# A chunked linear-attention kernel: state kept block-diagonal, TensorE's tile modes counted in the order of work, and spare matmuls at the start

## The chip, the cores and the metric

The kernel runs on one core of one Trainium2 chip. The metric is the device time of one launch in microseconds. The kernel before takes 105.71 us, the median of three runs (104.99 to 107.63). The profile was taken in another run of the same kernel, which took 102.53 us and whose profiled span is 100.8 us.

## The reference

Two parts follow each other. The first is a linear attention with a decaying state, for 4 sequences, 8 heads, 768 steps and head size 48. The second sends each of the 3072 resulting rows of 384 numbers through the best two of eight small adapters.

```python
def _attn_ref(r, k, v, w, u):
    state = zeros((B, H, D, D))
    for t in range(S):
        cur = einsum('bhd,bhe->bhde', u[None] * kt, vt)
        y[:, :, t] = einsum('bhd,bhde->bhe', rt, state + cur)
        state = wt[:, :, :, None] * state + einsum('bhd,bhe->bhde', kt, vt)

def _moe_ref(x, w_gate, A, B):            # E = 8 adapters of rank 16
    logits = x @ w_gate
    topk = the two largest;  w = softmax over those two
    out = x + sum over the two of  w * ((x @ A[e]) @ B[e])
```

The kernel handles a sequence as six tiles of 128 steps, 24 tiles in all. Within a tile, with cumulative sums of log w, the output has three terms: what the tile's own earlier steps give (a masked 128 by 128 matrix per head), what the state at the tile's start gives, and the diagonal term with u.

## The kernel before

Each step of the work is a small function of a tile number, and a long list, PLAN, gives the order in which all of them are issued; every engine then runs its own instructions in that order. A star in PLAN lets a copy change sides between ScalarE and VectorE. The host lays r and k out with head dimension on partitions, two heads to a tile of 128 partitions: head 0 of a pair in partitions 0 to 47, head 1 in 64 to 111.

The steps that matter here, with cuts marked:

```python
def cs(t):      # cumulative sums of log w: full-array matmuls, 4 or 8 of 128 columns
    ...
def expP(t):    # eP = exp(cs) on ScalarE; expN: exp(-cs)
def multR(t):   # rT = r * eP, multK: kT = k * eN, both on VectorE
def rku(t):     # r * k on GpSimd; dg(t): its sum with u by 4 matmuls of 2 columns
def dgev(t):    # dg of two tiles copied out of PSUM by ScalarE
def dv(t):      # v * dg on GpSimd: the diagonal term

def load_v(t):
    n = VGROUPS[t]
    v16 = io.tile([L, n, HD], FP16, name=f"v16_{t}")
    nc.gpsimd.dma_start(out=v16, in_=v[:, t:t + n])
    ...

def amm(t):     # a_ps[s, head, t] = k . r, 8 matmuls on 48 rows of the array
    ...
def aev(t):     # at = a_ps * mask, on VectorE

def kv(t):      # the state's sum over tiles, in PSUM
    if t % NC == 0:
        nc.tensor.matmul(S_acc, lhsT=zeros[:, 0:128], rhs=zeros, start=True, stop=False, ...)
    for p in range(P):
        for g in range(2):
            b = g * 64
            nc.tensor.matmul(S_acc[b:b + D, p], lhsT=st[t]["kn"][:, 2 * p + g], rhs=st[t]["v16"][:, 2 * p + g],
                             start=False, stop=True, ...)

def sev(t):     # the state copied to SBUF
    sb = wk.tile([128, P, D], BF16, name="S_sb", bufs=3)
    copy("ACT", sb, S_acc)
    st[t]["S"] = sb

def ymm(t):     # the three terms of the output
    y_ps = ring([128, P, 128], F32, "y_ps")
    s_ = st[t]
    for p in range(P):                                     # diagonal term
        nc.tensor.matmul(y_ps[:, p, :], lhsT=pair(s_["dv"], p), rhs=ident16, start=(p == 0), stop=False, ...)
    if t % NC > 0:
        for p in range(P):
            for g in range(2):                             # state's term
                b = g * 64
                nc.tensor.matmul(y_ps[b:b + D, p, :], lhsT=st[t - 1]["S"][b:b + D, p], rhs=s_["rT"][b:b + D, p], ...)
    for p in range(P):
        for g in range(2):                                 # the tile's own steps
            b = g * 64
            nc.tensor.matmul(y_ps[b:b + D, p, :], lhsT=s_["v16"][:, 2 * p + g], rhs=s_["at"][:, g * P + p], ...)
    s_["y_ps"] = y_ps

# yev: y_ps to xT (ScalarE); lg: gate logits; gate, gmax, gsel, z, zw, zT, zTev: the two best adapters,
# their weights and the first projection, for batches of 4, 4, 4, 4, 4, 3 and 1 tiles;
# d: x plus the second projection; oev: copy to SBUF; store: to DRAM
```

Memory for sums: [...] One bank, s_ps, is shared by the state (192 columns), dg (a slot for each of 24 tiles) and the gate logits lg (16 slots). The tiles kn_ps, y_ps, z_ps, zT_ps and d_ps take turns in two banks ("ring"). Input tiles have 12 buffers for r and k, 8 for w, and one of its own for every group of v.

Of the kernel before, what the change touches and what calls it, by code (L numbers as in the profile page):

```python
# [8 lines left out]
F32 = mybir.dt.float32  # L9
# [16 lines left out]
    setup.0 load_wb.0 adapters.0 load_wa.0 ln1.0 ln.0 cs.0 load_rk.0 expN.0 expP.0 casts.0 rku.0 multK.0 cs.1  # L26
    load_w.2 load_rk.1 ln.2 kT.0 load_rk.2 load_w.4 load_v.0 multR.0 expN.1 amm.0 expP.1 cs.2 multK.1 multR.1 dg.0
    expP.2 aev.0 load_rk.3 kT.1 load_v.1 rku.1 expN.2 dg.1 amm.1 dgev.1 ln.4 kev.1* multR.2 cs.3 kev.0 dv.0 expP.3
    multK.2 ymm.0 kT.2 kv.0 load_rk.4 rku.2 aev.1 expN.3 dg.2 multR.3 cs.4 amm.2 load_w.6 rku.3 load_rk.5 yev.0
    load_rk.6 sev.0 dv.1 multK.3 kv.1 dg.3 kev.2* load_v.4 expN.4 kT.3 dgev.3 dv.2 aev.2 expP.4 ymm.1 kev.3* sev.1  # L30
    amm.3 dv.3 cs.5 multK.4 rku.5 multR.4 yev.1 lg.0 lg.1 expN.5 aev.3 kv.2 expP.5 ymm.2 amm.4 load_w.8 ln.6 multK.5
    cs.6 adapterB.0 load_rk.7 multR.5 kT.4 yev.2 rku.4 sev.2 expP.6 dg.5 load_rk.8 rku.6 aev.4 ymm.3 multR.6
    load_w.10 kv.3 dg.4 expN.6 lg.2 kev.4* dgev.5 amm.5 dv.4 load_rk.9 multK.6 cs.7 sev.3 dg.6 kv.4 yev.3 lg.3 kT.6
    expN.7 ymm.4 gate.3 expP.7 sev.4 dv.5 aev.5 amm.6 kev.6 gmax.3 aev.6 ln.8 load_rk.11 kv.6 ymm.5 yev.4 cs.8
    load_rk.10 gsel.3 multK.7 sev.6 load_w.12 rku.7 multR.7 z.3 castB.0 yev.5 dg.7 expN.8 kT.7 zw.3 multK.8 expP.8
    amm.7 dgev.7 rku.8 dv.6 multR.8 load_v.8 load_rk.12 cs.9 aev.7 dg.8 load_w.14 kev.7* ln.10 dv.7 kT.8 expN.9
    expP.9 load_rk.13 multK.9 ymm.6 lg.5 kv.7 kev.8* amm.8 cs.10 sev.7 yev.6 rku.9 multR.9 aev.8 expN.10 lg.4
    multK.10 lg.6 zT.3 expP.10 multR.10 ymm.7 dg.9 zTev.3* cs.11 load_w.16 yev.7 amm.9 expN.11 aev.9 load_rk.14
    rku.11 rku.10 ln.12 lg.7 load_rk.15 dg.11 dg.10 expP.11 d.1 load_v.12 dgev.9 gate.7 dv.8 multK.11 kT.9 dv.9
    load_rk.16 kev.9* oev.1 cs.12 expN.12 amm.10 kv.8 kT.10 gmax.7 ymm.8 multR.11 dgev.11 gsel.7 load_rk.17 rku.12  # L40
    kev.10 multK.12 d.0 sev.8 kv.9 expP.12 multR.12 yev.8 cs.13 z.7 sev.9 oev.0 aev.10 ln.14 rku.13 ymm.9 zw.7 lg.8
    dv.10 expN.13 rku.14 dv.11 amm.11 expP.13 zT.7 cs.14 multK.13 zTev.7 yev.9 multR.13 ln.16 kT.13 load_w.20 kv.10
    d.3 lg.9 expN.14 load_w.18 dg.13 kev.13 expP.14 oev.3 ymm.10 aev.11 yev.10 multK.14 dg.12 kT.12 cs.15 amm.12 d.5
    sev.10 multR.14 kev.12* aev.12 dgev.13 rku.15 dg.14 ymm.11 expN.15 oev.5 lg.10 d.2 amm.13 kv.12 load_rk.18
    expP.15 dg.15 dv.13 multK.15 yev.11 oev.2 dv.12 sev.12 rku.16 kT.14 multR.15 cs.16 dgev.15 kev.14* load_v.16
    kv.13 kT.15 load_rk.19 lg.11 aev.13 expP.16 ymm.12 load_rk.20 kev.15 expN.16 amm.14 load_rk.22 gate.11 d.6
    load_rk.21 rku.17 sev.13 cs.17 dg.16 multR.16 yev.12 oev.6 multK.16 d.7 expP.17 ymm.13 gmax.11 gsel.11 oev.7
    kv.14 dv.15 z.11 expN.17 aev.14 multK.17 sev.14 amm.15 dv.14 yev.13 ln.18 dg.17 d.4 kv.15 zw.11 kT.16 oev.4
    load_w.22 cs.18 load_rk.23 multR.17 zT.11 sev.15 dgev.17 aev.15 kev.16* rku.18 expN.18 zTev.11 ymm.14 amm.16
    expP.18 ymm.15 multK.18 dg.18 cs.19 ln.20 yev.14 dv.16 lg.14 yev.15 kT.18 kv.16 multR.18 expN.19 lg.13 lg.12  # L50
    dv.17 aev.16 lg.15 d.10 kev.18* amm.17 load_v.20 expP.19 multK.19 ymm.16 cs.20 rku.19 sev.16 store.5 aev.17
    oev.10 rku.20 multR.19 gate.15 d.9 yev.16 gmax.15 expN.20 ymm.17 oev.9 kv.18 store.9 gsel.15 expP.20 store.2
    yev.17 multK.20 amm.18 d.8 oev.8 dg.19 cs.21 kT.19 store.3 dgev.19 aev.18 sev.18 expN.21 z.15 kev.19* dv.18
    amm.19 ymm.18 multR.20 expP.21 yev.18 lg.16 kv.19 zw.15 ln.22 zT.15 multK.21 rku.21 dg.21 dg.20 kT.21 zTev.15
    kev.21* aev.19 d.13 store.1 lg.18 multR.21 cs.22 kT.20 oev.13 sev.19 dv.19 kev.20 rku.23 amm.20 expN.22 ymm.19
    dgev.21 d.15 rku.22 store.6 dv.20 aev.20 lg.17 store.7 expP.22 dg.22 yev.19 multR.22 dg.23 kv.20 d.12 oev.15
    lg.19 amm.21 oev.12 dv.21 gate.19 multK.22 dgev.23 dv.23 sev.20 ymm.20 d.11 store.13 store.0 yev.20 oev.11
    aev.21 cs.23 store.10 dv.22 expN.23 gmax.19 kv.21 d.14 oev.14 sev.21 amm.22 ymm.21 yev.21 gsel.19 aev.22 z.19
    ymm.22 lg.20 multK.23 lg.21 expP.23 zw.19 yev.22 zT.19 lg.22 store.4 store.15 gate.22 store.12 multR.23 kT.22
    zTev.19 amm.23 d.17 kev.22* gmax.22 kv.22 aev.23 gsel.22 store.8 oev.17 d.18 sev.22 z.22 oev.18 zw.22 ymm.23  # L60
# [23 lines left out]
def kernel(  # L84
# [190 lines left out]
    def dg(t):  # L275
        for p in range(P):
            nc.tensor.matmul(dg_ps[:, t, 2 * p:2 * p + 2], lhsT=st[t]["rku"][:, p], rhs=w16[:, p, ER + E:],  # L277
                             start=False, stop=True, skip_group_check=True)
# [47 lines left out]

    def sev(t):
        sb = wk.tile([128, P, D], BF16, name="S_sb", bufs=3)
        copy("ACT", sb, S_acc)
        st[t]["S"] = sb  # L330

    def ymm(t):
# [5 lines left out]
        if t % NC > 0:  # L338
            for p in range(P):
                for g in range(2):  # L340
                    b = g * 64
                    nc.tensor.matmul(y_ps[b:b + D, p, :], lhsT=st[t - 1]["S"][b:b + D, p], rhs=s_["rT"][b:b + D, p],  # L342
                                     start=False, stop=False, skip_group_check=True)
# [156 lines left out]
```

## Time and profile before

| | us | share of the span |
|---|---|---|
| span of the profiled run | 100.8 | |
| TensorE matmul (PE) busy, 1505 matmuls | 85.9 | 85% |
| TensorE weight load (PEld) busy | 64.6 | 64% |
| ScalarE (ACT) busy | 72.3 | 72% |
| VectorE (DVE) busy | 72.0 | 71% |
| GpSimd (POOL) busy | 57.4 | 57% |
| DMA, moved | 25.19 MB | 250 GB/s in the mean |

Busy time of TensorE is a union of overlapping matmuls whose ends are modelled, so it says that TensorE had something under way, not that it streamed at its peak. In the profile's groups a matmul bears the rows and columns of the array that it uses: 128\*128 is the whole, 48\*128 the k and r products of one head, 128\*48 those with v of one head as weights, 48\*48 the state's term of one head. The granted clock has no record before about 5 us, and the page prints full speed there; the eight spare matmuls of 512 columns that the kernel already has at its start stand 0.43 us apart in the timeline.

The largest single groups are the masked copy of the attention matrix on VectorE (24 times 1218 ns), r times k on GpSimd (24 times 1088 ns) and the copies and exponentials of 128x512 on ScalarE (about 590 ns each, 72 of them).

### The profile page before, as it was taken

Reading aid. Unit: us, or ns where it says so; the run is one execution under the profiler, and the core shown is the slowest. Engines: PE = TensorE matmul, PEld = TensorE weight load, DVE = VectorE, ACT = ScalarE, POOL = GpSimd, SP = SyncE. Lnnn points to the kernel's source line nnn. Section 1 sums busy time; section 2 is a strip of 40 time slices with the busy share of each in tenths; the row PEclk is TensorE's granted clock in tenths of the full one; section 3 lists DMA queues with packets and bytes.
Section 4 is the critical chain, followed back from the end, with each engine's and each line's share of the span. In section 5 each row is a group of like instructions: output and inputs, shape, how many; then the busy total and the mean of one; then the engine's idle time right before and its main releaser. Section 6 shows DMA issues by size and latency. Waiting matters only on the chain.

```text
span 100.8 us, 3702 instructions
## 1 busy us (share of the span) xinstructions
PE 85.9 (85%) x1505; PEld 64.6 (64%) x1505; DVE 72.0 (71%) x145; ACT 72.3 (72%) x165; POOL 57.4 (57%) x95
## 2 busy tenths in 40 slices
PE   3935672999999998957999999999999999999840
PEld 1313661778588787735887788767787777866520
DVE  6205697076688989997689979896987995984410
ACT  5243583574859998994998899899887977465730
POOL 6105706959406989708995965996159849021300
PEclk9996555555579999999999999999999999999999
DMA  2999999999999999999998355009075285304272
GB/s 60 266 304 367 420 362 299 408 411 327 350 420 404 419 418 409 299 353 293 380 418 328 125 56 110 0 0 147 15 266 205 85 300 205 128 6 156 112 260 100
DMA packets 10097, 25.19 MB, mean 250 GB/s; under 512 B 1120, under 2 KB 4704, under 8 KB 10080
## 3 DMA queue, kind: packets, MB, share of 16 engines
q1 hardware_dynamic: 9072, 22.60, 58.9%
q0 software_dynamic: 1008, 2.36, 13.2%
q8 instruction: 11, 0.18, 0.7%
q14 instruction: 6, 0.05, 0.2%
HBM read 22.60 MB, written 4.72 MB: 271 GB/s over the span
## 4 chain that ended last, share of the span: by engine, by line
PE 68%; DMA 15%; POOL 5%; ACT 4%; DVE 2%; issue 1%; SPq 1%; DVEq 0%; POOLq 0%
DMA v<-in_v_dram 8%; PE y_ps L347 8%; PE a_ps L298 7%; PE y_ps L336 7%; PE y_ps L342 7%; DMA rk_in<-in_rk_dram 6%; PE z_ps L393 6%; PE d_ps L425 5%; PE cs_ps L238 5%; PE cs_ps L240 5%; PE kn_ps L310 4%; PE s_ps L324 4%; PE d_ps L427 3%; PE s_ps L358 2%; POOL rku L272 2%; PE s_ps L277 2%
## 5 line engine op out<-in xcount | busy, mean ns | idle before, releaser
L304 DVE TENSOR_TENSOR at<-a_ps,at_mask 128x1024 f16<-128x1024 f32 x24 | 29.2, 1218 | 7.4 <-PE a_ps L298 7.4
L288 POOL TENSOR_TENSOR dv<-v,dg 128x384 f16<-128x384 f16 x24 | 19.6, 828 | 17.1 <-ACT dg L282 8.4
L272 POOL TENSOR_TENSOR rku<-rk_in 128x512 f16<-128x512 f32 x24 | 25.7, 1088 | 5.8 <-DMA rk_in<-in_rk_dram 5.8
L119 ACT CAST xT<-y_ps 128x512 f16<-128x512 f32 x24 | 14.2, 593 | 9.2 <-PE y_ps L347 9.1
L262 DVE TENSOR_TENSOR kT<-rk_in,eN 128x512 bf16<-128x512 f32 x24 | 16.3, 679 | 6.1 <-DMA rk_in<-in_rk_dram 4.2
L258 DVE TENSOR_TENSOR rseq<-rk_in,eP 128x512 bf16<-128x512 f32 x24 | 16.3, 678 | 0.3 <-ACT eP L244 0.3
L247 ACT ACTIVATE eN<-cs_ps 128x512 f32<-128x512 f32 x24 | 14.2, 593 | 2.1 <-PE cs_ps L240 2.0
L244 ACT ACTIVATE eP<-cs_ps 128x512 f32<-128x512 f32 x24 | 14.2, 590 | 2.1 <-PE cs_ps L240 2.1
L240 PE MATMUL cs_ps<-incl,logw 128*128 128x128 f16 x96 | 14.5, 239 | 0.9 <-ACT logw L212 0.9
L238 PE MATMUL cs_ps<-co_excl,logw 128*128 128x128 f16 x80 | 12.6, 237 | 1.9 <-ACT eP L244 1.9
L119 ACT COPY res<-d_ps 128x384 f32<-128x384 f32 x24 | 11.5, 484 | 2.7 <-PE d_ps L427 2.5
L336 PE MATMUL y_ps<-ident,dv 128*128 128x128 f16 x96 | 10.1, 233 | 2.4 <-POOL dv L288 2.4
L240 PEld LDWEIGHTS <-logw 128*128 128x128 f16 x96 | 9.8, 107 | 3.4 <-issue 1.7
L298 PE MATMUL a_ps<-rseq,kT 48*128 48x128 bf16 x192 | 10.6, 236 | 0.7 <-DVE at L304 0.7
L220 ACT ACTIVATE logw<-w_in 128x768 f16<-128x768 f32 x11 | 9.4, 853 | 1.6 <-DMA w_in<-in_w_dram 1.6
L347 PE MATMUL y_ps<-at,v 128*48 128x128 f16 x192 | 10.4, 234 | 0.0
L238 PEld LDWEIGHTS <-logw 128*128 128x128 f16 x80 | 8.2, 106 | 2.5 <-ACT eP L244 1.3
L310 PE MATMUL kn_ps<-ident,kT 128*128 128x128 bf16 x80 | 8.8, 241 | 1.0 <-DVE rseq L253 0.8
L336 PEld LDWEIGHTS <-dv 128*128 128x128 f16 x96 | 6.5, 103 | 3.8 <-POOL dv L288 2.8
L382 POOL TENSOR_TENSOR g<-ge,top 128x32 f32<-128x32 f32 (+2 forms) x7 | 1.7, 236 | 12.4 <-DVE top L374 7.3
L342 PE MATMUL y_ps<-rseq,S_sb 48*48 48x128 bf16 x160 | 8.5, 229 | 0.0
L298 PEld LDWEIGHTS <-kT 48*128 48x128 bf16 x192 | 6.3, 101 | 3.3 <-issue 1.8
(64 smaller groups left out, 142.8 us busy)
## 6 DMA issues: line engine op xcount, KB each, us to landing
rk_in<-in_rk_dram SPq DMA_DIRECT2D x24, 516.0 KB, 11.1
out_dram<-res SPq DMA_DIRECT2D x24, 192.0 KB, 2.3
w_in<-in_w_dram SPq DMA_DIRECT2D x11, 384.0 KB, 11.4
v<-in_v_dram POOLq DMA_DIRECT2D x5, 384.0 KB, 8.0
w_in<-in_w_dram SPq DMA_DIRECT2D x2, 192.0 KB, 3.3
v<-in_v_dram POOLq DMA_DIRECT2D x1, 288.0 KB, 8.3
w_sb<-in_weights_dram SPq DMA_DIRECT2D x1, 276.0 KB, 2.8
B_sb<-in_moe_B_dram SPq DMA_DIRECT2D x1, 192.0 KB, 10.9
```

The source lines that it names most:

```text
L119: nc.scalar.copy(out=out, in_=in_)
L238: nc.tensor.matmul(cs_ps[:, p], lhsT=pair(st[t - 1]["logw"], p), rhs=co_excl, start=False, stop=False, skip_group_check=True)
L240: nc.tensor.matmul(cs_ps[:, p], lhsT=pair(st[t]["logw"], p), rhs=incl, start=False, stop=True, skip_group_check=True)
L258: nc.vector.tensor_mul(st[t]["rseq"][:, :, a + 1:a + 129], st[t]["rk"][:, 0, :, 1:129], eP)
L262: nc.vector.tensor_mul(st[t]["kT"], st[t]["rk"][:, 1, :, 1:129], eN)
L272: nc.gpsimd.tensor_mul(p_, st[t]["rk"][:, 0, :, 0:128], st[t]["rk"][:, 1, :, 1:129])
L288: nc.gpsimd.tensor_mul(dv_[:, :, 0:D], st[t]["v16"], st[t]["dg"].rearrange("p (h o) -> p h o", o=1).to_broadcast([L, H, D]))
L298: nc.tensor.matmul(a_ps[:, g, p, :], lhsT=k_[b:b + D, p, :], rhs=rT[b:b + D, p, :], start=True, stop=True, skip_group_check=True)
L304: nc.vector.tensor_mul(at, st[t]["a_ps"].rearrange("s g p f -> s (g p) f"), at_mask.to_broadcast([128, H, 128]))
L336: nc.tensor.matmul(y_ps[:, p, :], lhsT=pair(s_["dv"], p), rhs=ident16, start=(p == 0), stop=False, skip_group_check=True)
L342: nc.tensor.matmul(y_ps[b:b + D, p, :], lhsT=st[t - 1]["S"][b:b + D, p], rhs=s_["rT"][b:b + D, p], start=False, stop=False, skip_group_che ...
L347: nc.tensor.matmul(y_ps[b:b + D, p, :], lhsT=s_["v16"][:, 2 * p + g], rhs=s_["at"][:, g * P + p], start=False, stop=True, skip_group_check ...
```

## The change

The change has three parts and comes with a new order of all the work.

1. The state is kept block-diagonal. In PSUM and in SBUF each pair of heads has a 128 by 128 block (96 columns in PSUM) with the two 48 by 48 states on its diagonal and zeros elsewhere. The state's term of the output is then one full-array matmul for a pair in place of two in corners of the array. The state's accumulator grows from 192 to 384 columns, so dg and lg shrink to 8 slots each that are used again. The SBUF copies are three constant tiles, whose padding is zeroed at the start.
2. The output step is split into yd (diagonal and state's term, both on the full array) and yA (the tile's own steps), so that an order can place them apart. The new PLAN came from a search in which changes of TensorE's tile mode have a cost.
3. Five spare matmuls (junk), 512 columns each, into a ring buffer that nobody reads, are placed among the first steps.

The core of the diff, without the PLAN and without the changed slot indices of dg, dgev and gate:

```diff
+    S_sbs = [const.tile([128, P, 2, 64], BF16, name=f"S_sb_{i}") for i in range(3)]
...
-    S_acc = s_ps[:, 0:P * D].rearrange("a (p e) -> a p e", p=P)
-    o = P * D
-    dg_ps = s_ps[:, o:o + NT * H].rearrange("a (c e) -> a c e", c=NT)
-    o += NT * H
-    LSLOT = 16
-    lg_ps = s_ps[:, o:o + LSLOT * E].rearrange("a (c e) -> a c e", c=LSLOT)
+    S_acc = s_ps[:, 0:HD].rearrange("a (p g e) -> a p g e", p=P, g=2)
+    NSLOT = 8
+    dg_ps = s_ps[:, HD:HD + NSLOT * H].rearrange("a (c e) -> a c e", c=NSLOT)
+    lg_ps = s_ps[:, HD + NSLOT * H:HD + NSLOT * (H + E)].rearrange("a (c e) -> a c e", c=NSLOT)
...
+        for x in S_sbs:
+            nc.vector.memset(x[:, :, :, D:64], 0.0)
...
+    def junk(t):
+        j_ps = ring([128, 512], F32, "j_ps")
+        nc.tensor.matmul(j_ps, lhsT=ones, rhs=cpos, start=True, stop=True)
...
     def kv(t):
         if t % NC == 0:
-            nc.tensor.matmul(S_acc, lhsT=zeros[:, 0:128], rhs=zeros, start=True, stop=False, skip_group_check=True)
+            nc.tensor.matmul(s_ps[:, 0:HD], lhsT=zeros[:, 0:128], rhs=zeros, start=True, stop=False,
+                             skip_group_check=True)
         for p in range(P):
             for g in range(2):
                 b = g * 64
-                nc.tensor.matmul(S_acc[b:b + D, p], lhsT=st[t]["kn"][:, 2 * p + g], rhs=st[t]["v16"][:, 2 * p + g],
+                nc.tensor.matmul(S_acc[b:b + D, p, g], lhsT=st[t]["kn"][:, 2 * p + g], rhs=st[t]["v16"][:, 2 * p + g],
                                  start=False, stop=True, skip_group_check=True)
     def sev(t):
-        sb = wk.tile([128, P, D], BF16, name="S_sb", bufs=3)
-        copy("ACT", sb, S_acc)
+        c = t % NC
+        sb = S_sbs[(t // NC * (NC - 1) + c) % 3]
+        copy("ACT", sb[:, :, :, 0:D], S_acc)
         st[t]["S"] = sb
-    def ymm(t):
+    def yd(t):
         y_ps = ring([128, P, 128], F32, "y_ps")
...
         if t % NC > 0:
             for p in range(P):
-                for g in range(2):
-                    b = g * 64
-                    nc.tensor.matmul(y_ps[b:b + D, p, :], lhsT=st[t - 1]["S"][b:b + D, p], rhs=s_["rT"][b:b + D, p],
-                                     start=False, stop=False, skip_group_check=True)
+                nc.tensor.matmul(y_ps[:, p, :], lhsT=st[t - 1]["S"][:, p].rearrange("a g e -> a (g e)"),
+                                 rhs=s_["rT"][:, p], start=False, stop=False, skip_group_check=True)
+        s_["y_ps"] = y_ps
+
+    def yA(t):
+        s_ = st[t]
+        y_ps = s_["y_ps"]
         for p in range(P):
             for g in range(2):
                 b = g * 64
                 nc.tensor.matmul(y_ps[b:b + D, p, :], lhsT=s_["v16"][:, 2 * p + g], rhs=s_["at"][:, g * P + p],
                                  start=False, stop=True, skip_group_check=True)
-        s_["y_ps"] = y_ps
```

The PLAN before and after, cut to its first steps and to the place of the fourth load of v (cuts marked):

```text
before: setup.0 load_wb.0 adapters.0 load_wa.0 ln1.0 ln.0 cs.0 load_rk.0 expN.0 expP.0 casts.0 rku.0 multK.0 cs.1
        load_w.2 load_rk.1 ln.2 kT.0 load_rk.2 load_w.4 load_v.0 multR.0 expN.1 amm.0 expP.1 cs.2 multK.1 multR.1 dg.0
        expP.2 aev.0 load_rk.3 kT.1 load_v.1 rku.1 expN.2 dg.1 amm.1 dgev.1 ... multK.2 ymm.0 kT.2 kv.0 ...
        ... amm.7 dgev.7 rku.8 dv.6 multR.8 load_v.8 load_rk.12 cs.9 ...
after:  setup.0 load_w.2 load_wa.0 ln.0 load_wb.0 load_rk.0 load_rk.1 ln1.0 cs.0 junk.8 ln.2 junk.5 adapters.0 junk.10
        expP.0 expN.0 cs.1 load_w.4 multK.0 load_v.0 junk.4 expN.1 multR.0 junk.9 rku.0 load_rk.2 load_rk.3 expP.1 rku.1
        casts.0* multK.1 amm.0 kT.0 multR.1 cs.2 kT.1 load_v.1 ... multR.2 yd.0 rku.3 ln.4 rku.2 kv.0 ... yA.0 ...
        ... yA.3 ln.8 expN.7 aev.4 kT.6 expP.7 cs.8 load_w.12 sev.3 multK.7 load_v.8 yev.3 amm.5 ...
```

More of the change, by code (lines that the diff above doesn't have):

```diff
@@ L25 @@
 PLAN = """
[L26 to L60, printed above, removed]
@@ L61 @@
-    d.16 yev.23 store.11 oev.16 zT.22 store.14 lg.23 gate.23 d.19 zTev.22 d.21 gmax.23 oev.19 gsel.23 d.22 oev.21
-    store.17 oev.22 z.23 zw.23 store.18 store.16 zT.23 store.19 zTev.23 d.20 store.21 store.22 oev.20 d.23 store.20
-    oev.23 store.23
+    setup.0 load_w.2 load_wa.0 ln.0 load_wb.0 load_rk.0 load_rk.1 ln1.0 cs.0 junk.8 ln.2 junk.5 adapters.0 junk.10
+    expP.0 expN.0 cs.1 load_w.4 multK.0 load_v.0 junk.4 expN.1 multR.0 junk.9 rku.0 load_rk.2 load_rk.3 expP.1 rku.1
+    casts.0* multK.1 amm.0 kT.0 multR.1 cs.2 kT.1 load_v.1 expN.2 expP.2 dg.0 dg.1 dgev.1 cs.3 aev.0 dv.0 amm.1
@@ new lines @@
+    kev.0 multK.2 multR.2 yd.0 rku.3 ln.4 rku.2 kv.0 kev.1 expN.3 load_rk.4 expP.3 multK.3 yA.0 multR.3 cs.4 dv.1
+    load_w.6 aev.1 kT.3 load_rk.5 yev.0 sev.0 kT.2 kv.1 load_rk.6 kev.3 expN.4 rku.4 dg.2 dg.3 expP.4 multK.4
+    multR.4 amm.2 dgev.3 aev.2 load_w.8 cs.5 kev.2* sev.1 load_rk.7 load_v.4 kv.2 expN.5 load_rk.8 load_w.10 yd.1
+    kT.4 dv.2 rku.5 dv.3 expP.5 yA.1 ln.6 amm.3 cs.6 load_rk.9 kev.4 yev.1 yd.2 sev.2 adapterB.0 rku.6 multK.5 dg.5
+    yA.2 kv.3 dg.4 expN.6 multR.5 expP.6 yev.2 load_rk.10 dgev.5 cs.7 aev.3 multK.6 multR.6 amm.4 yd.3 yA.3 ln.8
@@ new lines @@
+    expN.7 aev.4 kT.6 expP.7 cs.8 load_w.12 sev.3 multK.7 load_v.8 yev.3 amm.5 dg.6 multR.7 load_rk.11 kev.6* rku.7
+    dg.7 lg.3 dv.4 expN.8 expP.8 kT.7 dv.5 lg.0 kv.4 lg.2 load_rk.12 lg.1 load_w.14 kev.7* gate.3 dgev.7 yd.4 aev.5
+    yA.4 multK.8 dv.6 amm.6 multR.8 sev.4 dv.7 aev.6 load_rk.13 cs.9 yev.4 ln.10 yd.5 kv.6 expN.9 yA.5 expP.9 yev.5
+    gmax.3 rku.9 yd.6 yA.6 yev.6 amm.7 cs.10 sev.6 kT.8 z.3 lg.6 multK.9 multR.9 kev.8* aev.7 dg.9 castB.0 kT.9
+    load_w.16 gsel.3 expN.10 zw.3 rku.8 kv.7 expP.10 amm.8 lg.4 rku.10 multK.10 dg.8 yd.7 kev.9* ln.12 dgev.9
@@ new lines @@
+    load_v.12 zT.3 sev.7 yA.7 aev.8 dv.9 dv.8 cs.11 zTev.3 multR.10 lg.5 yev.7 amm.9 kv.8 load_rk.14 rku.11 expN.11
+    load_rk.15 expP.11 d.1 oev.1 kT.10 load_rk.16 lg.7 dg.10 aev.9 kev.10* cs.12 yd.8 gate.7 multK.11 multR.11 yA.8
+    sev.8 rku.12 expN.12 amm.10 gmax.7 gsel.7 yev.8 kv.9 d.2 expP.12 dg.11 oev.2 d.0 rku.13 lg.8 cs.13 multK.12
+    kT.12 oev.0 sev.9 aev.10 expN.13 kev.12 yd.9 kv.10 yA.9 ln.14 z.7 yev.9 multR.12 multK.13 load_rk.18 amm.11
+    dgev.11 zw.7 load_rk.17 expP.13 kT.13 dv.10 dg.12 dg.13 cs.14 kev.13* zT.7 aev.11 dgev.13 ln.16 yd.10 zTev.7
@@ new lines @@
+    yA.10 amm.12 load_w.18 sev.10 expN.14 multR.13 dv.11 load_w.20 dv.12 yd.11 rku.14 aev.12 yA.11 yev.10 expP.14
+    kv.12 yev.11 d.7 amm.13 multR.14 oev.7 d.4 cs.15 multK.14 sev.12 oev.4 aev.13 lg.10 expN.15 lg.11 lg.9 dg.14 d.5
+    expP.15 yd.12 load_v.16 oev.5 rku.15 yA.12 multK.15 amm.14 dg.15 dv.13 kT.14 rku.16 load_rk.19 load_rk.20 yev.12
+    load_rk.22 multR.15 cs.16 aev.14 gate.11 dgev.15 d.3 kev.14* yd.13 gmax.11 kv.13 expN.16 oev.3 expP.16 dv.14
+    yA.13 amm.15 lg.12 dg.16 gsel.11 rku.17 yev.13 sev.13 multK.16 multR.16 d.6 oev.6 load_w.22 cs.17 aev.15 expN.17
@@ new lines @@
+    z.11 lg.13 zw.11 multK.17 yd.14 expP.17 load_rk.21 ln.18 yA.14 kv.14 load_rk.23 multR.17 dg.17 kT.16 yev.14
+    sev.14 rku.18 dgev.17 dv.15 store.1 cs.18 kT.15 kev.16 amm.16 load_v.20 dv.17 store.7 expN.18 kev.15 store.3
+    dg.18 lg.14 store.5 aev.16 expP.18 zT.11 yd.15 dv.16 yA.15 zTev.11 kv.15 cs.19 ln.20 multK.18 yev.15 sev.15 d.9
+    multR.18 rku.19 amm.17 lg.15 store.0 oev.9 expN.19 d.8 yd.16 aev.17 gate.15 yA.16 multK.19 kv.16 oev.8 expP.19
+    store.2 dg.19 kT.18 gmax.15 yev.16 dgev.19 kev.18* amm.18 rku.20 cs.20 sev.16 kT.19 kev.19* multR.19 expN.20
@@ new lines @@
+    z.15 gsel.15 dv.18 yd.17 expP.20 aev.18 yA.17 yev.17 kv.18 rku.22 ln.22 zw.15 lg.16 rku.21 multK.20 dg.20 zT.15
+    rku.23 d.10 cs.21 zTev.15 oev.10 d.11 multR.20 yd.18 dv.19 amm.19 expN.21 yA.18 sev.18* expP.21 kv.19 dg.22
+    oev.11 multK.21 aev.19 cs.22 dg.21 kT.21 yev.18 d.15 dgev.21 lg.18 dg.23 expN.22 dv.20 oev.15 amm.20 kev.21
+    multR.21 kT.20 sev.19 yd.19 dgev.23 yA.19 kev.20* kv.20 expP.22 aev.20 d.12 cs.23 multK.22 yev.19 sev.20 amm.21
+    store.9 oev.12 expN.23 dv.21 yd.20 lg.19 lg.17 multR.22 expP.23 store.8 store.10 gate.19 aev.21 store.11
@@ new lines @@
+    multR.23 yA.20 dv.22 yd.21 yev.20 gmax.19 yA.21 store.6 kv.21 kT.22 amm.22 yev.21 kev.22* gsel.19 lg.20 sev.21
+    multK.23 store.4 d.14 z.19 aev.22 dv.23 oev.14 yd.22 yA.22 zw.19 kv.22 store.15 lg.21 zT.19 yev.22 amm.23
+    store.12 sev.22* d.13 zTev.19* aev.23 lg.22 d.16 oev.13 gate.22 gmax.22 oev.16 d.19 oev.19 store.14 gsel.22
+    yd.23 yA.23 store.13 z.22 yev.23 lg.23 d.17 gate.23 zw.22 gmax.23 store.16 zT.22 zTev.22 oev.17 gsel.23 d.18
+    d.22 oev.18 d.20 oev.22 oev.20 z.23 zw.23 zT.23 store.19 zTev.23 d.21 store.17 oev.21 store.18 store.22 store.20
@@ L64 @@
+    store.21 d.23 oev.23 store.23
 """
@@ L172 @@
     ones = const.tile([128, 128], FP16, name="ones")
-    zeros = const.tile([128, 192], FP16, name="zeros")
+    zeros = const.tile([128, HD], FP16, name="zeros")
     cpos = const.tile([128, 512], FP16, name="cpos")
     logws = [const.tile([L, 2, H, 64], FP16, name=f"logw_{i}") for i in range(3)]
+    S_sbs = [const.tile([128, P, 2, 64], BF16, name=f"S_sb_{i}") for i in range(3)]
     dvs = [const.tile([L, H, 64], FP16, name=f"dv_{i}") for i in range(4)]
@@ L200, in setup @@
         make_upper_triangular(nc, at_mask[:, 0, :], val=1.0, diag=False)
-        nc.tensor.matmul(S_acc, lhsT=zeros[:, 0:128], rhs=zeros, start=True, stop=True, skip_group_check=True)
+        nc.tensor.matmul(s_ps[:, 0:HD], lhsT=zeros[:, 0:128], rhs=zeros, start=True, stop=True, skip_group_check=True)
         for i in (1, 2):
@@ L276, in dg @@
         for p in range(P):
-            nc.tensor.matmul(dg_ps[:, t, 2 * p:2 * p + 2], lhsT=st[t]["rku"][:, p], rhs=w16[:, p, ER + E:],
+            nc.tensor.matmul(dg_ps[:, t % NSLOT, 2 * p:2 * p + 2], lhsT=st[t]["rku"][:, p], rhs=w16[:, p, ER + E:],
                              start=False, stop=True, skip_group_check=True)
@@ L281, in dgev @@
         dg_ = wk.tile([L, 2, H], F32, name="dg", bufs=3)
-        nc.scalar.copy(out=dg_, in_=dg_ps[:, t - 1:t + 1, :])
+        q = t % NSLOT
+        nc.scalar.copy(out=dg_, in_=dg_ps[:, q - 1:q + 1, :])
         for i in range(2):
@@ L357, in lg @@
         for p in range(P):
-            nc.tensor.matmul(lg_ps[:, t % LSLOT, :], lhsT=st[t]["xT"][:, p, :], rhs=w16[:, p, ER:ER + E],
+            nc.tensor.matmul(lg_ps[:, t % NSLOT, :], lhsT=st[t]["xT"][:, p, :], rhs=w16[:, p, ER:ER + E],
                              start=False, stop=(p == P - 1), skip_group_check=True)
@@ L362, in gate @@
         t0, n = gate_at[t]
-        q = t0 % LSLOT
+        q = t0 % NSLOT
         ge = wk.tile([L, GMAX, E], F32, name="ge")[:, 0:n, :]
```

## The prediction

> **What bounds the kernel now.** I read the page's slices first, then a table of stages, then the timeline inside a stage, then the waits. The slices (40 of 2.52 us) show three stretches: TensorE half busy up to about 17 us, then nearly always busy, then a tail of some 8 us.
>
> ```profile
> PE   3935672999999998957999999999999999999840
> ACT  5243583574859998994998899899887977465730
> PEclk9996555555579999999999999999999999999999
> ```
>
> The third row is the clock granted to TensorE: half from slice 4 to slice 10. Cutting the stage table at the changes of that clock gives, per row, length, then PE, PEld, DVE, ACT and POOL busy time with counts, then clock, DMA share and GB/s:
>
> ```profile
> 8.46:17.00 8.54, 4.61 (x52) 3.66 (x50) 7.39 (x12) 5.14 (x10) 4.38 (x6) 0.50 1.05 373
> 17.00:28.94 11.94, 11.94 (x157) 8.95 (x158) 6.28 (x9) 6.93 (x16) 8.05 (x9) 0.50 1.04 375
> 28.94:93.00 64.06, 61.49 (x1244) 48.09 (x1242) 54.81 (x107) 53.69 (x129) 42.16 (x65) 1.00 0.66 226
> 93.00:100.80 7.80, 3.13 (x38) 1.90 (x36) 1.36 (x6) 3.10 (x8) 0.84 (x4) 0.99 0.42 152
> ```
>
> From 17.0 us on TensorE is the bound: busy for all of 11.94 us at half clock and for 61.49 of the next 64.06 at full clock. VectorE and ScalarE follow at 54.81 and 53.69 of 64.06, that is 86% and 84%, so they would bind soon after it. Before 17 us nothing is dense; there the inputs set the pace. A busy TensorE isn't a TensorE at its peak, so the next view is the timeline of a stage at full clock (start, length of the group, idle before it in brackets):
>
> ```profile
> 51.69 0.22 PE L238 MATMUL cs_ps<-co_excl,logw 128*128 128x128 f16 x1
> 51.74 0.22 PE L240 MATMUL cs_ps<-incl,logw 128*128 128x128 f16 x1
> ...
> 52.89 0.38 PE L336 MATMUL y_ps<-ident,dv 128*128 128x128 f16 x4
> 53.21 0.41 PE L342 MATMUL y_ps<-rseq,S_sb 48*48 48x128 bf16 x8
> 53.54 0.41 PE L347 MATMUL y_ps<-at,v 128*48 128x128 f16 x8
> 53.88 0.25 PE L277 MATMUL s_ps<-w,rku 128*128 128x2 f16 x4
> ```
>
> Two full-array matmuls of 128 columns start 0.055 us apart, so four take 0.22 us. The four of L336 take 0.32 us before L342 starts. The eight of L342 sit in two corners of the array and run in pairs, so they should also take four slots, 0.22 us, yet L347 starts 0.33 us later; L347 takes 0.34 us. At each place where the used part of the array changes (128*128, 48*48, 128*48, 128*128) some 0.10 us is lost in which nothing streams. That is the cost the change aims at.
>
> The waits show a second loss. ScalarE-made and DMA-made waits of GpSimd reach TensorE at two places:
>
> ```profile
> 9.68 1.31 POOL L146 DMA_DIRECT2D v<-in_v_dram  x2
> 11.01 1.11 POOL L272 TENSOR_TENSOR rku<-rk_in 128x512 f16<-128x512 f32 x1
> 16.07 0.83 POOL L288 TENSOR_TENSOR dv<-v,dg 128x384 f16<-128x384 f16 x1 [3.95 <-ACT eN L247]
> ...
> 37.11 0.61 POOL L146 DMA_DIRECT2D v<-in_v_dram  x1
> ...
> 45.73 1.61 POOL L288 TENSOR_TENSOR dv<-v,dg 128x384 f16<-128x384 f16 x2 [3.47 <-DMA v<-in_v_dram]
> ```
>
> The load of v for tiles 8 to 11 is issued at 37.11 and its first user starts at 45.73. The chain of waits has the same stretch as one 8.47 us piece of DMA. Around it TensorE starts nothing for 0.83 us after 43.1, 0.98 after 44.6 and 0.58 after 46.0, less the matmul itself about 2.1 us. At the start the first dv stands at 16.07, named after ScalarE, whose eN had long been done; the v of tile 0, issued at 9.68 with 6.2 us to landing, fits 15.9.
>
> [...]
>
> **The change part by part.**
>
> *State matmuls.* For 20 tiles (all but the first of each sequence) eight 48*48 matmuls become four 128*128 ones in the same mode as the dv matmuls before them. 0.33 us becomes 0.22 us: 20 x 0.11 = 2.2 us off TensorE.
>
> *Order.* I put each matmul of both instruction orders into its mode and counted the changes: 143 before, 101 after. Twenty of the 42 are in the item above. 22 x 0.10 = 2.2 us more. The split of ymm into yd and yA lets yA stand beside kv, which has its mode. Sum for TensorE: 4.4 us at full clock, of some 76 us in which it binds.
>
> *The state's copy.* It grows from 128x192 to 128x384. The rows that size it:
>
> ```profile
> L119 ACT CAST S_sb<-s_ps 128x192 bf16<-128x192 f32 x20 | 6.6, 329 | 1.1 <-PE s_ps L277 1.1
> L119 ACT COPY res<-d_ps 128x384 f32<-128x384 f32 x24 | 11.5, 484 | 2.7 <-PE d_ps L427 2.5
> ```
>
> So I take 484 instead of 329 ns. Eighteen stay on ScalarE: 18 x 0.155 = 2.8 us more, less two copies moved away (2 x 0.329), less two kn copies that go to VectorE (2 x 0.49), plus the weights cast that comes to it (about 0.6): 72.3 + 1.8 = 74.1 us. VectorE gains about 1.6 us. In 28.94 to 93, two thirds of the span, ScalarE rises from 53.7 to about 55 us while TensorE's 61.5 falls by some 3.7 to under 58. The two come close together; with queues in order and single buffers between them, I let half of the 4.4 us show: **2.2 us**.
>
> *Order of the v loads.* The new order issues v of tile 0 ahead of the first rku, and v of tiles 8 to 11 after rku.6 where it was after dv.6. In the trace before, rku.6 ended at 26.3 us, so the load may go out some 10 us earlier and land before it is needed. I count **2.2 us**: 2.1 plus the smaller delays around it. At the start dv.0 can run about 3 us earlier, but v of tiles 1 to 3 is still issued after rku.1, near 11 us, and lands near 19; TensorE only gets a little more done before that: **0.8 us**.
>
> *Spare matmuls.* Five of 512 columns (0.43 us at half clock) stand in the places where TensorE idles before 17 us (gaps of 1.3, 1.4, 1.0 and 1.1 us before 11.4 us), so they cost little. Their worth lies in the clock. The dense half-clock part is 11.94 us; at full clock TensorE could do it in some 6.5, but GpSimd was busy 8.05 and ScalarE 6.93 of it, so 8.0 us is the floor and 3.9 us is there to win. [...] The runs without a profile are 104.99 to 107.63, the profiled one 102.53, so I suspect that they stay slow for longer still, which leaves more to win. I count **3.3 us**.
>
> *Memory of the sums.* dg and lg keep 8 slots instead of 24 and 16. A slot is read within about 4 tiles, so I see no wait: 0.
>
> Sum: 2.2 + 2.2 + 0.8 + 3.3 = 8.5 us; 105.7 - 8.5 = 97.2, taken as **97.0 us**.
>
> **The rivals.**
>
> *ScalarE takes over.* It had 84% in the dense stretch, and the wider state copy stands between kv and the next tile's state matmul. For it: the 2.8 us above. Against it: TensorE still has more to do. If it wins, the 4.4 us shrink to under 1 and the time is about 98.5.
>
> *The clock stays as it was.* The spare matmuls are over before 13 us[...]. Then only 5.2 us remain: 100.5.
>
> *The clock never falls.* [...] GpSimd and the inputs set the stretch to 29 us. Then also the worse runs of before are avoided: 93 to 94.
>
> *The new order costs elsewhere.* A re-searched order may bring a late load or a longer tail. The tail (7.80 us with TensorE busy 3.13) is a chain from gate to store that nothing here shortens. A loss of 2 to 3 us would put the time near 100.
>
> **Range and chances.** The clock is the widest term, 0 to 6 us, the rest perhaps 2 us either way: 92.5 to 102.0. Within 2% means 103.6 or more; for that nearly all terms must fail. Slower by 2% would take a new wait larger than all gains.
>
> **What would show it.** State matmuls: four 128*128 at 0.055 us, no gap of 0.10 us between dv's and theirs. Order: TensorE busy 4 us less for the same tiles. Copy: S_sb near 484 ns, ScalarE near 74 us. v: no wait of dv for the DMA in tiles 8 and 9. Clock: full rate before 24 us. It would be wrong if the clock stays at half to 29 us or later, if TensorE's idle time for ScalarE grows by more than 2 us, or if v of tiles 1 to 3 lands later than 19 us.

## The result and the profile after

The changed kernel takes 92.43 us (median of four runs, 92.19 to 93.30) where the kernel before took 105.35 us beside it (104.44 to 107.63). The ratio is 0.8818, with a 95% interval of 0.8736 to 0.8899; ratios here compare only those runs of each kernel that lie near its fastest, medians are of all runs. The predicted 97.0 us was too cautious: the measured time stands just below the lower end of its range, 92.5. Taken between the two profiled runs, the gain is 9.2 us (102.53 to 93.30).

The profiled run of the changed kernel has a span of 91.6 us against 100.8. Its slices (40 of 2.29 us):

```profile
PE   2996866069999999999999999999999999997740
DVE  5203989904999999999999999999999999873210
ACT  5056879237699999999999999999989998475640
PEclk9999999855699999999999999999999999999995
```

Counted from 0, three engines are now full from slice 11 to about slice 30, not TensorE alone; and the stretch of half clock covers three slices in place of seven. The table of stages, cut again where the clock changes (length, then PE, PEld, DVE, ACT and POOL busy with counts, clock, DMA share, GB/s):

```profile
7.42:17.66 10.24, 6.01 (x96) 4.39 (x95) 8.76 (x16) 7.41 (x15) 5.67 (x6) 1.00 1.05 369
17.66:24.49 6.83, 5.31 (x70) 3.95 (x71) 3.16 (x5) 3.62 (x8) 5.26 (x7) 0.50 1.02 413
24.49:80.00 55.51, 55.37 (x1161) 46.40 (x1159) 54.28 (x105) 53.02 (x124) 42.10 (x62) 1.00 0.80 272
80.00:91.60 11.60, 6.77 (x95) 4.35 (x89) 3.77 (x14) 5.48 (x13) 1.81 (x8) 0.90 0.42 155
```

In the third row VectorE has 98% and ScalarE 96%, where they had 86% and 84% of the dense stretch before. The groups' time hardly differs; the stretch around them became shorter.

A piece of the timeline of TensorE at full clock shows the new output step:

```profile
60.07 0.39 PE L345 MATMUL y_ps<-ident,dv 128*128 128x128 f16 x4
60.30 0.39 PE L349 MATMUL y_ps<-rseq,S_sb 128*128 128x128 bf16 x4
60.61 0.41 PE L359 MATMUL y_ps<-at,v 128*48 128x128 f16 x8
60.85 0.27 PE L332 MATMUL s_ps<-v,kn 128*48 128x48 f16 x8
```

The four dv matmuls take 0.23 us until the state's begin: no gap. The state's take 0.31 us with the change to 128*48 behind them. The tile's own steps are followed by the state update in the same mode, after 0.24 us where it was 0.34.

Where the 9.2 us between the two profiles went can be read from one landmark, the masked copy of the attention matrix on VectorE, for the tiles with numbers 5 and 20, first before and then after:

```profile
30.61 1.22 DVE L304 TENSOR_TENSOR at<-a_ps,at_mask 128x1024 f16<-128x1024 f32 x1 [0.35 <-PE a_ps L298]
...
80.07 1.22 DVE L304 TENSOR_TENSOR at<-a_ps,at_mask 128x1024 f16<-128x1024 f32 x1
```

```profile
29.34 1.22 DVE L311 TENSOR_TENSOR at<-a_ps,at_mask 128x1024 f16<-128x1024 f32 x1
...
72.02 1.22 DVE L311 TENSOR_TENSOR at<-a_ps,at_mask 128x1024 f16<-128x1024 f32 x1
```

Up to tile 5 the changed kernel is ahead by 1.3 us. The fifteen tiles between take 42.7 us in place of 49.5, 6.8 us less, all at full clock in both. The rest to the end takes 18.4 in place of 19.5, counted from the ends of the copies. Inside the fifteen tiles I went through the starts of all matmuls: tile-mode changes fall from 91 to 62, some 2.7 us at 0.092 us each; the state's term from 3.2 to 2.7 us; and the time in which TensorE starts nothing, beyond what the stream and the changes need, from 3.5 to 0.2 us. These make 6.5 us; the remaining 0.3 us is work, cumulative sums above all, that the new order has outside these tiles.

The v loads and their users on GpSimd, after:

```profile
10.82 0.60 POOL L147 DMA_DIRECT2D v<-in_v_dram  x1
12.36 0.82 POOL L295 TENSOR_TENSOR dv<-v,dg 128x384 f16<-128x384 f16 x1 [0.94 <-ACT dg L289]
...
19.20 0.83 POOL L295 TENSOR_TENSOR dv<-v,dg 128x384 f16<-128x384 f16 x1 [2.93 <-DMA v<-in_v_dram]
...
25.30 0.59 POOL L147 DMA_DIRECT2D v<-in_v_dram  x1
...
38.22 1.61 POOL L295 TENSOR_TENSOR dv<-v,dg 128x384 f16<-128x384 f16 x2 [0.52 <-ACT dg L289]
```

The load for tiles 8 to 11 goes out at 25.30 and nobody waits for it. The load for tiles 1 to 3 still ends the one long wait of the start: dv of tile 1 at 19.20, and TensorE idle for 3.3 us before 19.18.

### The profile page after: what moved, and what is told of

It reads as the page before. It is cut to its first block, busy times and chain, and to the rows that moved or that the text cites. A ratio compares the mean times of both kernels' runs of the same rounds, so it can differ in the third digit from the quotient of the medians.

```text
span 91.6 us, 3552 instructions
## 1 busy us (share of the span) xinstructions
PE 79.2 (87%) x1430; PEld 61.3 (67%) x1430; DVE 71.8 (78%) x151; ACT 72.7 (79%) x162; POOL 57.6 (63%) x95
## 4 chain that ended last, share of the span: by engine, by line
PE 68%; DMA 17%; ACT 4%; issue 3%; SPq 2%; DVE 2%; POOL 0%; DVEq 0%
DMA v<-in_v_dram 9%; PE a_ps L305 8%; DMA rk_in<-in_rk_dram 8%; PE y_ps L359 8%; PE z_ps L404 6%; PE y_ps L345 6%; PE d_ps L436 5%; PE cs_ps L244 5%; PE y_ps L349 5%; PE cs_ps L246 5%; PE kn_ps L317 4%; PE d_ps L438 4%; PE s_ps L332 4%; PE s_ps L369 3%; PE s_ps L283 3%
## 5 line engine op out<-in xcount | busy, mean ns | idle before, releaser
L244 PE MATMUL cs_ps<-co_excl,logw 128*128 128x128 f16 x80 | 11.5, 224 | 2.1 <-ACT eP L250 1.2
L246 PE MATMUL cs_ps<-incl,logw 128*128 128x128 f16 x96 | 13.3, 227 | 0.0
L246 PEld LDWEIGHTS <-logw 128*128 128x128 f16 x96 | 9.4, 102 | 2.8 <-issue 2.1
L305 PE MATMUL a_ps<-rseq,kT 48*128 48x128 bf16 x192 | 10.0, 226 | 0.3 <-DVE rseq L264 0.3
L345 PE MATMUL y_ps<-ident,dv 128*128 128x128 f16 x96 | 9.5, 223 | 0.1
L244 PEld LDWEIGHTS <-logw 128*128 128x128 f16 x80 | 7.7, 99 | 2.3 <-ACT eN L253 1.6
L120 ACT CAST S_sb<-s_ps 128x384 bf16<-128x384 f32 x18 | 9.1, 506 | 0.0
L332 PE MATMUL s_ps<-v,kn 128*48 128x48 f16 x160 | 5.7, 189 | 3.3 <-DMA v<-in_v_dram 3.3
L436 PE MATMUL d_ps<-ident,xT 128*128 128x96 f16 x96 | 8.0, 206 | 0.2
L349 PE MATMUL y_ps<-rseq,S_sb 128*128 128x128 bf16 x80 | 8.0, 224 | 0.0
L317 PE MATMUL kn_ps<-ident,kT 128*128 128x128 bf16 x80 | 7.8, 224 | 0.0
```

What stands on the lines that cost most here:

```text
L120: nc.scalar.copy(out=out, in_=in_)
L244: nc.tensor.matmul(cs_ps[:, p], lhsT=pair(st[t - 1]["logw"], p), rhs=co_excl, start=False, stop=False, skip_group_check=True)
L246: nc.tensor.matmul(cs_ps[:, p], lhsT=pair(st[t]["logw"], p), rhs=incl, start=False, stop=True, skip_group_check=True)
L305: nc.tensor.matmul(a_ps[:, g, p, :], lhsT=k_[b:b + D, p, :], rhs=rT[b:b + D, p, :], start=True, stop=True, skip_group_check=True)
```

## The experiments

Twelve kernels ran, the changed one once more among them, in three sets of four; within a set they ran on one chip beside the kernel before. The theory: the gain is the sum of TensorE time removed, of idle time removed and of half-clock time removed. The rivals are that ScalarE takes the gain back, that the spare matmuls and the clock are most of it, or that a wait only changes its place.

### The spare matmuls alone, and the change without them

```diff
 # b_junk: the PLAN of the kernel before
-cs.0 ... cs.1
+cs.0 junk.8 junk.5 junk.10 ... cs.1 junk.4 junk.9
 # a_nojunk: the PLAN after, all five junk steps taken out
```

> The kernel before plus the five spare matmuls only (three behind the first cumulative sum, two behind the second), order and state as before. Theory 1, in which the gain is a sum of TensorE time removed, idle time removed and slow clock removed: the clock falls later or for a shorter stretch, and 3 to 4 us go, 105.3 to about 102. Rival, in which the spare matmuls and the clock are most of the gain: about 97. Second rival, in which the slow stretch is ended by the denser work and not by the spare matmuls: 105, with the clock at half until 28 us or later as before.

> The changed kernel without the five spare matmuls, all else kept. Theory 1: the clock falls early and returns after the dense work starts near 19 us; TensorE waits for v of tile 1 until then anyway, so the loss is 1 to 2 us, about 94. Rival, the spare matmuls are most of the gain: 98 or more. Second rival, they do nothing: 92.4.

The kernel before with spare matmuls: 106.32 us (104.44 to 106.55) beside 103.83 (101.16 to 106.17). The changed kernel without them: 91.78 us (91.32 to 92.36; ratio 0.9058, interval 0.8921 to 0.9195 to the kernel before in its set). The spare matmuls bring no gain in either kernel. In the second profile the clock indeed falls early, as this table of stages of the kernel without them shows, and no cost of it can be seen:

```profile
8.27:21.93 13.66, 11.13 (x137) 9.21 (x137) 10.64 (x17) 9.10 (x19) 9.17 (x11) 0.50 1.04 387
21.93:80.00 58.07, 57.74 (x1194) 47.86 (x1193) 56.62 (x108) 55.38 (x129) 43.76 (x64) 1.00 0.81 279
```

Half clock from 8.27 to 21.93 us lies where the first inputs set the pace. The profile of the first kernel shows something else, a second fall in the middle:

```profile
30.00:47.00 17.00, 14.93 (x316) 11.94 (x314) 15.37 (x31) 15.55 (x37) 10.63 (x15) 1.00 1.04 386
47.05:53.88 6.83, 6.74 (x77) 5.23 (x79) 3.15 (x6) 3.88 (x9) 6.52 (x11) 0.50 1.04 363
```

It comes behind a stretch in which TensorE was busy for 14.93 of 17.00 us, and across it the run loses 2.7 us against the profile of before, which has none.

### The block-diagonal state alone

```diff
 # b_diag: all of the change but its PLAN; in the PLAN of before
-ymm.t
+yd.t yA.t
```

> The kernel before in its own order with the block-diagonal state only (wide state copy, eight slots for dg and lg; the diagonal and state's term and the tile's own steps back to back as before): tile-mode changes 123 in place of 143, no spare matmuls. Theory 1, TensorE binds and all of its saved time shows: 20 x 0.11 = 2.2 us less, about 103. Rival, ScalarE takes over because its state copy grows from 329 to 506 ns: 105 or more, with ScalarE's idle time gone and TensorE waiting for the state copy.

99.41 us (99.05 to 100.29), ratio 0.9834 (0.9714 to 0.9954): 1.7 us against the better runs of before, near the 2.2 expected, and 4.4 us between the medians. Its profile, 2.8 us shorter than that of before, has most of this elsewhere than expected: the fifteen tiles take 48.8 us, only 0.7 less (13 changes fewer are worth 1.2 us, but TensorE idles 0.3 us more), while the copy of tile 5 begins 1.6 us earlier, half clock having ended at 24.8 in place of 28.9 us. So it is partly luck that the gain comes near 2.2. ScalarE's copy is the one row that grew:

```profile
L119 ACT CAST S_sb<-s_ps 128x384 bf16<-128x384 f32 x20 | 9.9, 494 | 1.3 <-PE s_ps L282 1.2
```

TensorE waits for it 0.6 us in all, so ScalarE doesn't take over and the rival falls. What I had not expected is that the spread is smaller: the four runs were granted clocks of 0.908 to 0.923, 1.2 us apart. The nine runs of before in the same set had 0.93 to 0.98 at 101.2 to 101.3 us, 0.886 at 103.5 to 103.8, and 0.856 to 0.868 at 105.4 to 106.2. In the other two sets the order is less clean: there two runs of before took 107.08 and 108.69 us at 0.988 and 0.980. This mean counts time without a clock record as full clock, so it can read too high: b_v8 below shows 0.991, though its 128-column matmuls stood 0.107 us apart until 24.3 us. My guess was that the block-diagonal state keeps the clock up, and that was to be tested.

### The load of v moved, both ways

```diff
 # b_v8: PLAN of before          # a_v8late: PLAN after
-rku.6 ... dv.6 multR.8 load_v.8 -multK.7 load_v.8 ... dv.6 ... rku.8
+rku.6 load_v.8 ... dv.6 multR.8 +multK.7 ... dv.6 ... rku.8 load_v.8
```

> The kernel before with one thing moved: the load of v for tiles 8 to 11 is issued behind rku.6 in place of behind dv.6. Theory 1: the idle time of TensorE between 37 and 46 us (about 2.1 to 2.6 us) goes and the time falls by as much, to about 103. Rival, in which another wait takes its place[...]: 105.

> The changed kernel with the load of v for tiles 8 to 11 put behind rku.8 and dv.6, where the kernel before has it. Theory 1: TensorE idles again near 40 us for 1.5 us or more, and ScalarE and VectorE, which are full there too, can't give it back: 94 to 95. Rival: the new order has slack there, under 93.

In the kernel before: 101.56 us (99.69 to 102.65), ratio 0.9898 (0.9684 to 1.0111), so in time alone the move doesn't stand clear of the spread; its effect is read from the profile. The idle time of TensorE in the fifteen tiles falls from 3.5 to 2.1 us; 0.8 us stay at 41.5, where the next sequence's first sums wait for the exponentials. So the move is worth some 1.4 us there, not 2.2, and no other wait took its place. In the changed kernel the late load costs 8.0 us in the median, 100.41 (97.94 to 100.70), and about 6 us between the best runs. Its timeline of TensorE:

```profile
38.54 0.40 PE L304 MATMUL a_ps<-rseq,kT 48*128 48x128 bf16 x8
44.70 0.36 PE L331 MATMUL s_ps<-v,kn 128*48 128x48 f16 x8 [5.76 <-DMA v<-in_v_dram]
```

TensorE stands idle for six microseconds, and half clock from 41.3 to 48.1 comes with it. The load was issued at 35.84, only 1.3 us before its time in the kernel before; but the order around it arrives at the need earlier, while from issue to first user the load takes 8.9 us, up to 44.70, where it took 8.6 in the kernel before. Both rivals fall; theory 1 had the idle time right in kind and four times too small.

### The state's term put back into the corners, and the output step joined again

```diff
 # a_corners: the order after, with the state's code of before
-nc.tensor.matmul(y_ps[:, p, :], lhsT=S[:, p] (128 columns), rhs=rT[:, p], ...)
+for g in range(2): nc.tensor.matmul(y_ps[b:b + D, p, :], lhsT=S[b:b + D, p], rhs=rT[b:b + D, p], ...)
 # a_joined: in the PLAN after, each yd.t taken out of its place
-yd.t ... yA.t
+... yd.t yA.t
```

> The changed kernel once more, as the measure for the three others of this set: 92 to 93.3 us as before.

> The changed kernel in its own order, with the state's term put back into the corners of the array (eight 48*48 matmuls per tile, state copy of 192 columns, 329 ns): 126 tile-mode changes in place of 101. Theory 1, TensorE binds and every change costs about 0.09 us: 25 x 0.09 = 2.3 us more, about 94.7. Rival, ScalarE binds as much as TensorE in the new order (it was busy 15.96 of 16 us in one stage): its copies get 18 x 0.17 = 3 us cheaper, which takes back most of the loss, under 93.5.

> The changed kernel with the first half of the output step moved down to stand directly ahead of its second half in every tile, all else kept: 110 tile-mode changes in place of 101. Theory 1: 9 x 0.09 = 0.8 us more, about 93.3, more if the ring buffers now make TensorE wait. Rival, the place of the two halves matters for the waits and not for the modes: 95 or more, with idle time of TensorE ahead of the diagonal term.

The changed kernel once more: 92.38 us (91.26 to 93.27). With corners: 97.15 us (94.38 to 97.46), 4.8 us more, twice the 2.3 expected; its best run against the best of the changed kernel differs by 3.1. Between tiles 5 and 20 it takes 43.7 us in place of 42.6, so the changes cost there about what they should. In the profile, which is of one of the longer runs (96.98 us), 2.3 us of the loss lie ahead of tile 5 and 1.3 us behind tile 20. The second part stays unexplained; the clock row of its page suggests what made the first:

```profile
PEclk9999755895569999999999999999999999999995
```

It has two stretches of half clock, 10.7 to 17.6 and 21.0 to 27.8 us, where the changed kernel in this set has one from 16.6 to 23.4. The cheaper copies of ScalarE gave nothing back.

Joined: 93.98 us (93.40 to 95.01), 1.6 us more. In the fifteen tiles there are 7 more changes (0.65 us) and 0.4 us more idle time, 43.8 us in all. The place of yA beside kv is worth its modes and a little slack; the rival with waits alone falls.

### Does the density of the stream hold the clock up?

```diff
 # b_spare: the kernel before, in ymm behind the diagonal term, for every tile
+        for p in range(P):
+            nc.tensor.matmul(y_ps[:, p, :], lhsT=zeros[:, 0:128], rhs=ident16, start=False, stop=False, ...)
```

> The kernel before with four more full-array matmuls of 128 columns in every tile, directly behind the diagonal term and in its mode, with zeros as weights, so that the sum stays the same; 96 in all, state's term in the corners as before, 143 tile-mode changes as before. Theory 1, [...] full clock comes before 28 us and doesn't fall again around 45 us, every run is granted 0.90 or more, and the time is the 101.3 us of the runs at good clock plus 24 x 0.22 = 5.3 us, less 1 to 2 us for the earlier clock: 105. Rival, [...] runs again spread over 5 us with clocks from 0.85 to 0.98, 106 to 112.

The kernel does 96 matmuls more, which add zero, and keeps the order, the changes and the waits. It takes 103.97 us (103.57 to 104.31), beside 105.78 (102.80 to 108.69) for the kernel before: lower in the median with 5.3 us more to do, and level with the best runs (ratio 1.0041, 0.9897 to 1.0184). Its stages:

```profile
20.30:45.00 24.70, 22.76 (x476) 18.37 (x475) 21.88 (x41) 22.08 (x52) 16.56 (x22) 1.00 1.04 373
45.00:93.00 48.00, 47.71 (x955) 37.99 (x953) 38.44 (x74) 37.42 (x88) 30.41 (x49) 1.00 0.52 169
```

Full clock from 20.3 us on (until then its 128-column matmuls stand 0.107 us apart), and no fall near 45 us although TensorE idles there nearly as before (0.83, 0.87 and 0.59 us between starts). The profile of before has no fall there either, so this pair of profiles doesn't decide between theory and rival. For theory 1 speak the earlier full clock and the four runs within 0.7 us, where the seven of before lie 5.9 us apart.

The traces of the kernel before and of the changed kernel can be divided further. Their clock records last 3.41 us or a multiple of it, but for the last of each: 3.41 at full clock, 20.48 at half and 71.68 at full in the one, 10.24, 6.83 and 64.85 in the other. I divided both into these steps of 3.41 us and took for each the share of time in which columns stream, at 0.42 ns a column (0.83 at half clock; from 512-column matmuls 0.215 and 0.427 us apart), what runs side by side counted once. Six steps at half clock were followed by half: their shares are 0.37, 0.57, 0.40, 0.72 and 0.75 before the change, 0.39 after it. One step of each trace was followed by full, both with 0.80. At full clock, twenty steps of each were followed by full, with 0.42 to 0.80, and two of each by half: 0.27 and 0.00 (the last, without a matmul) before the change, 0.25 and 0.29 after it. The page's busy time doesn't separate the steps at half clock: two of the six that stayed were busy throughout, as were the two that left. This is read off two traces and wasn't put to a run of its own; what the clock follows is not shown by it.

### A better start

```diff
 # a_v1:   PLAN after, load_v.1 moved directly behind load_v.0
 # a_v1w:  a_v1, and adapters.0 moved ahead of load_rk.1
 # a_start: PLAN after without junk;
-setup.0 load_w.2 load_wa.0 ln.0 load_wb.0 load_rk.0 load_rk.1 ... ln.2 ... adapters.0 ... rku.1 ... load_v.1
+setup.0 load_wa.0 load_wb.0 ln.0 load_rk.0 load_w.2 adapters.0 load_rk.1 ... expN.0 ln.2 ... rku.0 load_v.1 ...
```

> The changed kernel with the load of v for tiles 1 to 3 issued directly behind that of tile 0, ahead of the first rku (about 3.7 us in place of 10.8 us). Theory 1: the wait of TensorE for this load (3.3 us before 19.2) goes for the most part, 90 to 91. Rival, the load takes the DMA engines from r and k of the first tiles, which land later: no gain, 92.4 or more.

> The changed kernel with v of tiles 1 to 3 issued directly behind v of tile 0, and the adapter weights issued ahead of r and k of tile 1. Theory 1: the wait that took the place of the one for v (ScalarE's cast of the adapter weights, 2.1 us) shrinks to under 0.5 us and 1 to 2 us go: 90.5 to 91.3. Rival, the first loads [...] only change places: 92 or more.

> The changed kernel without spare matmuls and with another start: the halves of w of tile 0 and r and k of tile 0 ahead of w of tile 2, the adapter weights ahead of r and k of tile 1, the logarithm of tile 2 behind the first exponentials, v of tiles 1 to 3 behind the first rku. Theory 1: r and k of tile 0 land near 6.4 us in place of 7.4, v of tiles 1 to 3 near 16 in place of 19: 89.5 to 90.5. Rival, in which the start isn't what sets the end, because ScalarE and VectorE are full from 29 us on: 91.5 or more.

a_v1: 92.84 us (91.07 to 94.76). a_v1w: 92.89 us (90.62 to 95.23; ratio 0.8781, 0.8487 to 0.9075). a_start: 94.14 us (93.48 to 94.31; ratio 0.9081, 0.8948 to 0.9213). None beats the changed kernel in the median. Two runs of a_v1w, 90.62 and 91.21 us, lie below all of the changed kernel's, the other two at 94.57 and 95.23; its profile is of the last. In a_v1 the wait for v of tile 1 is gone, and ScalarE's cast of the adapter weights waits 2.1 us for its load instead; its best runs are no better than those of the changed kernel in the same set. In a_start tile 5 ends 2.4 us earlier than in the first profile of the changed kernel (28.1 us in place of 30.6), and by tile 7 it is 0.5 us behind. Its waits between 26 and 31 us (who waited for whom, total, times, longest) say why:

```profile
POOL dv L294 <- DMA v<-in_v_dram: 3.1, 1, 3.1
PE s_ps L331 <- DMA v<-in_v_dram: 1.8, 1, 1.8
```

The start runs ahead into the load of v for tiles 4 to 7, which was placed for the slower start; TensorE idles, and the clock falls to half from 30.7 to 34.1. In a_v1w the same happens from 28.7 to 35.5. Theory 1 fails for a_start and for the medians of the other two: the start's gain turns into a new wait. For the better runs of a_v1w, which are at its forecast, that is not shown. A version with that load earlier too wasn't run.

## Why the prediction was too cautious

**The bound.** Right. TensorE was the bound, and mode changes were what it lost. 143 changes became 101, and the sum of 4.4 us for TensorE was sized well: in the fifteen tiles, 15/24 of the tiles, 3.2 of 4.4 us were found.

**"I let half of the 4.4 us show."** This step failed. All of it showed in the fifteen tiles: TensorE's idle time there went down to 0.2 us, so the 3.2 us alone exceed the 2.2 counted for all tiles; what the 4.4 came to over the whole span wasn't measured. ScalarE and VectorE at 96% and 98% still follow without making it wait. That is the order's doing: with the same state in the old order (b_diag) the idle time stayed at over 3.5 us. Their busy shares of 84% and 86% before were no sign of a second bound; they were the result of TensorE's pace.

**The state's copy.** Sized well at 484 ns (measured 494 and, in the changed kernel, 506):

```profile
L120 ACT CAST S_sb<-s_ps 128x384 bf16<-128x384 f32 x18 | 9.1, 506 | 0.0
```

TensorE never waited for it, GpSimd once for 1.8 us. ScalarE's busy time rose to 72.7 us only, not 74.1, although its instructions' lengths add up to 87.1 us in place of 84.2, 3.0 more: they overlap in the timeline, and busy time counts such stretches once.

**The v loads.** Right in kind, short in size. The move of the one load is worth 1.4 us in the old order; the new order removed 3.3 us of idle time in the fifteen tiles, where I had counted 2.2. At the start dv of tile 0 ran at 12.36 in place of 16.07 and v of tiles 1 to 3 came at 19.2, as foreseen. The 0.8 us for it isn't visible by itself: tile 1's masked copy ended 0.9 us later than before.

**The clock.** The 3.3 us were my estimate, with nothing in the trace of before to show that spare or denser matmuls end half clock, and they went in part to the wrong cause. The spare matmuls bring no gain. Full clock came at 24.5 in place of 28.9 us, just behind the 24 set as a sign, and is probably most of the 1.3 us at tile 5: the kernel before with only its load moved went to full clock at 24.3, and there the masked copy of tile 5 began at 29.0 us, in the order of before. The rest lies in runs other than the profiled one, a part that the prediction named as a suspicion. Most runs of the kernel before take 103 to 109 us where its best take 101.2. The clocks of the first set, the second fall in b_junk and the steadier runs of b_diag and b_spare point to more time at half clock in those runs. That is my estimate and isn't shown: of such runs in the old order only that of b_junk has a trace. The books close like this: 9.2 us between the two spans, plus 2.8 us by which the median of before exceeds its profiled run (105.35 - 102.53), plus 0.9 us by which that of the changed kernel falls short of its own (93.30 - 92.43), make the 12.9 us between the medians. So between the profiles the gain, 9.2 us, is close to the 8.5 of the sum, and most of what was missing from the number, 3.7 us, lies in which runs were taken. That closeness is partly luck: the halved term and the idle time were counted too small, the 1.1 us behind tile 20 had no term, and the clock's 3.3 us stand against at most 1.3 ahead of tile 5.

**The rivals.** ScalarE takes over: no. The clock stays as it was: no. The clock never falls, 93 to 94 us: the time was reached although the clock did fall, at a place where the inputs set the pace. The new order costs elsewhere: no, with its spare matmuls and moved loads it was worth more than the state alone. The change with the old order stands at 99.4 us, the new order with the old state at 97.2, both together at 92.4.

## What to carry to other kernels

Count the places where the used part of TensorE's array changes, in the order of issue; at 0.09 us each they cost 0.4 of four full-array matmuls (0.22 us) here, and a wider matmul half full of zeros that stays in mode was the cheaper one (diagonal and state's term 0.54 us in place of 0.65). Busy shares of 85% on the other engines were no reason to halve what is removed from the bound, once the order was searched anew. What speeds up one part can need the next loads moved as well: twice here a start that ran ahead, and once a load placed later, ended in a wait for v.
